# A fused attention backward on one core: normalised o kept in the rows of do, wide projections and transposes, a later dv

## The chip, the core and the metric

The kernel runs on one core of a Trainium2 chip. Five engines work side by side, each through its own queue in order: PE (TensorE, matmuls; its weight loads are listed as PEld), DVE (VectorE), ACT (ScalarE), POOL (GpSimd) and SP (SyncE, which here only issues DMAs). The metric is device time of one execution in microseconds, lower is better.

## The reference

Two attention blocks run on separate inputs, their outputs are laid side by side, and the kernel returns that output and the gradients of all inputs for a given `grad_out`. S = 2048 tokens, D = 448, H = 16 heads of 28 columns, bf16.

```python
# block A: linear attention
qkv = (x @ wqkv) -> q, k, v          # per head
pq, pk = phi(q), phi(k)              # phi(t) = where(t > 0, t + 1, exp(t)) + 1e-6
kv = einsum("bhsd,bhse->bhde", pk, v); z = sum of pk over the tokens
a = (pq @ kv) / (pq . z + 1e-6) @ wo

# block B: multi-query attention, one k and one v for all heads
q = x @ wq; k = x @ wk; v = x @ wv
p = softmax(q k^T * Dh**-0.5)
b = (p v) @ wo

out, vjp = jax.vjp(concat(a, b)); return out, vjp(grad_out)
```

What the change touches is block B. With o = p v (per head, normalised), do = (gradient of b) wo^T and D = rowsum(do * o), its backward needs dv = p^T do, ds = p * (do v^T - D), dq = ds k, dk = ds^T q, the gradient of wo, which is o^T (gradient of b), and the projections of dq, dk, dv.

## The kernel before

Phase A (to about 200 us) computes all of block A. A preparation of block B (`phase_B_pre`) makes q, k and v; q in rows of tokens (`qn`, in the memory of the tile that the trace calls gaT) is stored to DRAM as `qn_d`. Then comes the main loop.

**Main loop.** It works on 64 blocks b; a block is 256 tokens of q (`qc = b // 8`) and two heads (`pair = b % 8`). Each block passes over all 2048 keys in 8 steps of 256 keys, so there are NU = 512 steps u. The program is written out by hand (`tc.manual_schedule`): one pass of `for u in range(NU + 28)` issues work of several ages.

- Scores of step u (`rows_SD`, PE) go to two of three PSUM banks SB; ACT turns them into e with two exps (L888, L932). e (`eT`) is not normalised.
- For w = u - 16, PE makes do v^T into the banks DB. DVE multiplies one head with e (L893); ACT copies the other (L895) and POOL multiplies it (L896). This is ds. DVE transposes it two steps later (L964).
- In odd u PE adds to dk (`dk_m`); in even u it adds to o and dq (`o_dq`) and to dv (`dv_mm`).
- dv needs e with keys and queries exchanged. SP does this by DMA, one `dma_start_transpose` of two steps at a time (L935), into one of 11 buffers `eN`. The four products of block b are issued in the even steps with u mod 8 of 2, 4, 4 and 6, the first one at u = 8b + 18.

Every matmul helper `mmt` places a product on a part of the array (`tile_position`); `mm` uses all of it. All of them appear in the profile as L627 (mmt) or L81 (mm).

**Once per block.** At u = 8b + 9 DVE copies o out of PSUM into `oTs` (L913). At u = 8b + 10 PE transposes it in eight narrow products per block (`onat_T`) into the `spare` bank of SB, which is the first bank that the scores of u + 1 need. `o_norm` then lets DVE copy it into SBUF (L769) and take the reciprocal of the row sums (L770). POOL multiplies them into the normalised `onat` (L774), scales do by the same factor into `don` (L778), and multiplies do with o (L783), which DVE sums to D two steps later. At u = 8b + 14 `don` is transposed for the next ds.

The identity of `onat_T` takes all 128 rows, so rows 64 to 128 of oTs are set to zero once, by a DVE memset at u = 4 (L906).

**Once per eight blocks.** `onat` (256 tokens, all heads) goes two ways: transposed by SP into `oTq` (L924) for the output projection (`out_proj`, in the steps with u mod 64 of 24, 32, 40, 48), and stored by POOL to a DRAM scratch `on_d` (L908). The q rows for dk are loaded by POOL from `qn_d`, four copies, one each at u mod 64 of 30, 38, 46 and 54 (for the first block at u = 2, 4, 6, 8).

**do.** `do_nat` holds do in rows of tokens. It is produced in slots inside the loop (`do_slots`: `do_proj` on PE, `do_copy` on DVE, L858), 20 of them before u = 27 and 12 up to u = 184, those with u a multiple of 8.

**End of the loop.** From u = 512 no scores are left. `post_load` loads the gradient rows (`gb`, L716), the stored o rows (`on`, L720) and the x rows (L727) through SP, into free eT and eN buffers. `gwo` multiplies o and gradient rows for the gradient of wo, in a count per step that the list `GW` gives, from u = 523. After the loop come the products for the gradients of wk, wv, wq and x.

Of the kernel before, what the change touches and what calls it, by code (L numbers as in the profile page):

```python
# [9 lines left out]
ALU = mybir.AluOpType  # L10
AX = mybir.AxisListType
BF16 = mybir.dt.bfloat16
F32 = mybir.dt.float32
# [11 lines left out]
def kernel(  # L25
# [44 lines left out]
    on_d = dpool.tile([S, 512], BF16, name="on_d")  # L70
# [536 lines left out]
    with ExitStack() as cs_:  # L607
        psA = psc.enter_context(tc.tile_pool(name="psAcc", bufs=1, space=bass.MemoryType.PSUM))
        pe_ = cs_.enter_context(tc.tile_pool(name="ceT", bufs=10, side="right"))
        pn_ = cs_.enter_context(tc.tile_pool(name="ceN", bufs=11, side="right"))  # L610
# [5 lines left out]
        pm_ = cs_.enter_context(tc.tile_pool(name="csm", bufs=2, side="right"))  # L616
# [7 lines left out]
        eT, eN, dsT, dsx, qX, onat, don, doT, rl, prod = ({} for _ in range(10))  # L624
# [37 lines left out]
        oTs = pm_.tile([P, 256], F32, name="oTs", bufs=1)  # L662
# [13 lines left out]
        def out_proj(i, c0, c1, ps):  # L676
            for c in range(4):
                for j in range(4):
                    js = slice(32 * j, 32 * j + 32)
                    mmt(ps[js, 0:c1 - c0], oTq[i // 2][:, 4 * (i % 2) + c, js], wo[:, c, c0:c1], (0, 32 * j), c == 0,  # L680
                        c == 3)
# [11 lines left out]
        post = {"gb": [], "on": [], "xb": []}  # L693
# [6 lines left out]
        def post_load(k):  # L700
            if k in (2, 4, 6, 8):
                zero(post["dkvT"][64:128, 256 * k - 512:256 * k])
            if k == 0:
                mix = pq_.tile([P, 4, 2, 512], BF16, name="qX").rearrange("p a b c -> p (a b c)")
                post["dkvT"], post["dkvn"], post["wkvT"] = mix[:, 0:2048], mix[:, 2048:3072], mix[:, 3072:3072 + D]
                zero(post["wkvT"][64:128, :])
                nc.sync.dma_start(post["wkvT"][0:64, :], wkvT_d[:, :])
            i = k % 4
# [5 lines left out]
            elif k < 4:  # L714
# [3 lines left out]
                n = 4 if i < 3 else 2  # L718
                t = by_tokens(pn_.tile([P, 16, P], BF16, name="eN").rearrange("p a b -> p (a b)"))
                nc.sync.dma_start(t[:, 0:n, :], on_d[i * 512:i * 512 + n * P, :].rearrange("(t p) d -> p t d", p=P))  # L720
                post["on"] += [t[:, j, :] for j in range(n)]
                if i == 3:
                    post["on"] += [onat[7][:, j, :] for j in range(2)]
# [6 lines left out]
        def gwo(n0, n1):  # L730
            for n in range(n0, n1):
# [4 lines left out]
                mm(al[:, 0:D], post["on"][st][:, g_ * P:(g_ + 1) * P], post["gb"][st][:, 0:D], start=(st == 0),  # L736
# [8 lines left out]
        GW = [0, 0, 0, 0, 4, 8, 12, 16, 19, 22, 26, 29, 32, 36, 40, 44, 48, 52, 56, 60, 64, 64]  # L745
# [6 lines left out]
        def onat_T(b, bank):  # L752
            onp = bank[:, 0:P].rearrange("p (q h c) -> p q h c", q=2, h=2)
            for qb in range(2):
                for j in range(4):
                    mmt(bank[32 * j:32 * j + 32, qb * 64:qb * 64 + 64], oTs[:, qb * P + 32 * j:qb * P + 32 * j + 32],
                        identF[:, 0:64], (0, 32 * j), True, True)
            onps[b] = onp

        def o_norm(b):  # L760
            onp = onps.pop(b)
            qc, pair, g, hp = blk(b)
            if pair == 0:
                onat[qc] = pm_.tile([P, 2, 512], BF16, name="onat")
            ont = onat[qc]
            cs0 = slice(pair * 64, pair * 64 + 64)
            r_ = pw_.tile([P, 2, 2, 1], F32, name="rl")
            os_ = oTs[:, 0:P].rearrange("p (q h c) -> p q h c", q=2, h=2)
            nc.vector.tensor_copy(out=os_, in_=onp[:, :, :, :])  # L769
            nc.vector.reciprocal(out=r_[:], in_=os_[:, :, :, 0:1])  # L770
            rl[b] = r_
            onv = ont[:, :, cs0].rearrange("p q (h c) -> p q h c", c=32)
            dnv = do_nat[:, 2 * qc:2 * qc + 2, cs0].rearrange("p q (h c) -> p q h c", c=32)
            nc.gpsimd.tensor_tensor(out=onv, in0=os_, in1=r_[:].to_broadcast([P, 2, 2, 32]),  # L774
                                    op=ALU.mult)
# [3 lines left out]

        def do_o(b):  # L780
            qc, pair, g, hp = blk(b)
            prod[b] = pw_.tile([P, 2, 2, 32], F32, name="prod", bufs=1)
            nc.gpsimd.tensor_tensor(  # L783
                out=prod[b][:],
                in0=do_nat[:, 2 * qc:2 * qc + 2, pair * 64:pair * 64 + 64].rearrange("p q (h c) -> p q h c", c=32),
                in1=onat[qc][:, :, pair * 64:pair * 64 + 64].rearrange("p q (h c) -> p q h c", c=32),
                op=ALU.mult)
# [63 lines left out]
        def do_proj(i, h, ps):  # L851
            for c in range(4):
                for j in range(4):
                    js = slice(32 * j, 32 * j + 32)
                    mmt(ps[js, 0:256], gbT[:, i, c, js], woTp[:, c, h * 256:(h + 1) * 256], (0, 32 * j), c == 0, c == 3)
# [7 lines left out]
        with tc.manual_schedule():  # L863
            tc.keep_in_program_order(nc.scalar.activation(out=ex[:], in_=ex[:], func=ACT.Exp))
            for u in range(NU + 28):
# [31 lines left out]
                if u in (2, 4, 6, 8) or u % 64 in (30, 38, 46, 54) and u < 448:  # L897
                    qc, a = (u // 64 + 1, (u % 64 - 30) // 8) if u > 20 else (0, (u - 2) // 2)
# [6 lines left out]
                if u == 4:  # L905
                    nc.vector.memset(oTs[64:128, :], 0.0)  # L906
                if (b := due(u, 14)) is not None and b % 8 == 7 and b < NB - 1:
# [35 lines left out]
                else:  # L943
                    o_dq((u - 2, u - 1), (u - 20, u - 19))
                    for n in {2: (0,), 4: (1, 2), 6: (3,)}.get(u % 8, ()):
                        if 0 <= (b := u // 8 - 2) < NB:
                            dv_mm(b, n // 2, n % 2)
# [120 lines left out]
```

## Time and profile before

| what | us |
|---|---|
| median of 4 runs | 1113.7 |
| lowest and highest of them | 1111.68 and 1118.39 |
| the profiled execution, its time | 1109.44 |
| its span in the profile | 1107.7 |
| main loop, u = 16 to 512 | 262 to 1027 |
| end of the loop, u = 512 to 540 | 1027 to 1071 |
| after the loop | 1071 to 1107.7 |

In the timelines shown below a row has the start in us from the span's beginning, the duration in us, the engine, the line of the kernel, the operation, what is written and read by the program's names, the shape, and how often the row stands for a run of the same kind. In brackets stand the idle time of the engine before it and what ended that time. In the view of one tile a row has minimum, median and maximum duration in ns, and first and last start in us.

### The profile page before, as it was taken

What the parts mean: (1) busy time and instruction counts of PE and PEld (TensorE: products, weight loads), DVE (VectorE), ACT (ScalarE), POOL (GpSimd) and SP (SyncE); (2) the same over time, 40 slices, a digit from 0 to 9 for tenths busy, and PEclk for the clock granted to TensorE, in tenths of its full rate; (3) what the DMA queues carried; (4) which work ended last, traced back from release to release, by engine and by line L of the source; (5) the groups of instructions that cost most, each with busy time, mean ns of one, the idle gap of its engine ahead of it and who ended that gap; (6) DMA issues with size and microseconds to landing.
All of it is one profiled execution on the core that took longest, in us unless ns stands there. A gap on an engine that the chain in (4) does not pass through costs nothing.

```text
span 1107.7 us, 42448 instructions
## 1 busy us (share of the span) xinstructions
PE 1046.6 (94%) x17285; PEld 502.6 (45%) x17285; DVE 892.9 (81%) x1773; ACT 876.6 (79%) x1744; POOL 768.1 (69%) x993
## 2 busy tenths in 40 slices
PE   9999999969999999999999999999899999999898
PEld 5545555435444444444444444444444444444344
DVE  7887400426999999999999999999999999899842
ACT  6453122448999999999999999999999999999521
POOL 6001242225898898889889898888898898888740
PEclk9999999979999999999999999999999999999999
DMA  9869899199999999999999999999999999999992
GB/s 268 147 121 171 171 186 222 34 204 196 182 197 183 187 193 187 187 192 188 190 179 203 193 186 188 191 190 174 194 197 193 197 186 194 178 184 175 248 210 63
DMA packets 674963, 202.89 MB, mean 183 GB/s; under 512 B 649760, under 2 KB 670288, under 8 KB 674768
## 3 DMA queue, kind: packets, MB, share of 16 engines
q1 hardware_dynamic: 662368, 177.03, 99.6%
q0 software_dynamic: 7440, 19.20, 6.7%
q10 hardware_dynamic: 4960, 3.96, 1.2%
q8 instruction: 135, 2.21, 0.8%
q14 instruction: 60, 0.49, 0.2%
HBM read 22.83 MB, written 14.77 MB: 34 GB/s over the span
## 4 chain that ended last, share of the span: by engine, by line
PE 69%; DVE 11%; ACT 10%; DMA 7%; issue 2%; POOL 0%; SPq 0%; DVEq 0%; ACTq 0%
PE dk_acc L627 19%; PE agen L81 13%; PE sps L627 12%; ACT eT L932 8%; PE oq L627 6%; PE dps L627 5%; DMA eN<-eT 5%; PE aacc L81 4%; PE dv_acc L627 4%; DVE dsT L893 3%; PE sps L81 3%; DVE dsx L964 3%; PE sps L800 1%; ACT cp L895 1%; DVE R L916 1%
## 5 line engine op out<-in xcount | busy, mean ns | idle before, releaser
L896 POOL TENSOR_TENSOR dsT<-cp,eT 128x512 bf16<-128x512 bf16 x512 | 589.6, 1157 | 105.0 <-ACT cp L895 93.4
L627 PEld LDWEIGHTS <-R 32*128 32x128 bf16 (+1 forms) x8704 | 227.5, 94 | 293.0 <-issue 259.3
L893 DVE TENSOR_TENSOR dsT<-dps,eT 128x512 bf16<-128x512 f32 x512 | 340.9, 666 | 24.2 <-PE dps L627 18.5
L964 DVE STREAM_TRANSPOSE dsx<-dsT 128x512 f32<-128x512 f32 x512 | 355.6, 695 | 2.1
L888 ACT ACTIVATE eT<-sps 128x512 bf16<-128x512 f32 x512 | 312.0, 609 | 38.0 <-PE sps L627 17.2
L895 ACT ACTIVATE cp<-dps 128x512 bf16<-128x512 f32 x512 | 312.7, 611 | 13.0 <-PE dps L627 11.9
L932 ACT ACTIVATE eT<-sps 128x512 bf16<-128x512 f32 x512 | 318.8, 623 | 0.0
L627 PE MATMUL dk_acc<-dsx,qX 32*32 32x512 bf16 x4096 | 267.6, 375 | 0.0
L627 PE MATMUL dps<-doT,R 32*128 32x256 bf16 x2048 | 247.8, 269 | 5.8 <-ACT cp L895 2.0
L627 PE MATMUL sps<-R,R 32*128 32x256 bf16 (+1 forms) x2240 | 226.3, 274 | 8.7 <-DVE R L858 1.9
L627 PE MATMUL oq<-eT,R 128*32 128x256 bf16 x2048 | 157.8, 275 | 0.0
L627 PE MATMUL oq<-dsT,R 128*32 128x256 bf16 x2048 | 156.3, 274 | 0.1
L627 PEld LDWEIGHTS <-qX 32*32 32x32 bf16 x4096 | 79.6, 89 | 114.5 <-issue 53.8
L627 PE MATMUL dv_acc<-eN,don 128*32 128x512 bf16 x1024 | 101.9, 379 | 7.2 <-DMA eN<-eT 7.0
L397 POOL MEMSET ga<- 64x448 bf16 x2 | 0.9, 470 | 95.7 <-DVE pr L348 82.5
L547 DVE TENSOR_TENSOR osb<-R 32x512 bf16<-32x512 bf16 x4 | 1.7, 413 | 62.1 <-ACT R L544 62.1
L81 PEld LDWEIGHTS <-R 128*128 128x128 bf16 (+1 forms) x361 | 29.5, 99 | 27.7 <-issue 5.6
L627 PE MATMUL sps<-identF,oTs 128*32 128x64 f32 x1024 | 27.6, 225 | 7.5 <-ACT eT L932 0.2
L627 PEld LDWEIGHTS <-don 128*32 128x32 bf16 x1024 | 34.3, 97 | 0.3
L901 POOL DMA_DIRECT2D qX<-qn_d x32 | 18.6, 581 | 16.8 <-DMA qn_d<-gaT 16.8
L774 POOL TENSOR_TENSOR onat<-oTs,rl 128x128 bf16<-128x128 f32 x64 | 25.7, 401 | 6.1 <-DVE rl L770 6.1
L81 PE MATMUL agen<-R,R 128*128 128x448 bf16 x128 | 28.6, 352 | 0.9 <-ACT R L220 0.6
(225 smaller groups left out, 1029.4 us busy)
## 6 DMA issues: line engine op xcount, KB each, us to landing
qX<-qn_d POOLq DMA_DIRECT2D x32, 256.0 KB, 5.1
eN<-eT SPq DMA_TRANSPOSE x256
out_dram<-osb ACTq DMA_DIRECT2D x22, 112.0 KB
qn_d<-gaT SPq DMA_DIRECT2D x2, 1024.0 KB
xa<-in_A_x_dram SPq DMA_DIRECT2D x8, 224.0 KB
ga<-in_grad_out_dram SPq DMA_DIRECT2D x4, 448.0 KB
xa<-in_grad_out_dram POOLq DMA_DIRECT2D x4, 448.0 KB, 6.6
out_dram<-wdq POOLq DMA_DIRECT2D x8, 224.0 KB, 3.6
```

Of the source, the lines that this page charges most:

```text
L81: nc.tensor.matmul(out_ap, lhsT=lhsT, rhs=rhs, start=start, stop=stop, tile_position=(0, 0))
L627: nc.tensor.matmul(out, lhsT=lhsT, rhs=rhs, start=start, stop=stop, tile_position=pos, skip_group_check=True)
L774: nc.gpsimd.tensor_tensor(out=onv, in0=os_, in1=r_[:].to_broadcast([P, 2, 2, 32]), op=ALU.mult)
L800: nc.tensor.transpose(tp2[q:q + 32, qb * P:(qb + 1) * P], don[b][:, qb, h, :], identB[:, :], tile_position=(0, q))
L888: nc.scalar.activation(out=et[:, u % 2, 0, :], in_=sp[0][:, :], func=ACT.Exp, scale=scale)
L893: nc.vector.tensor_tensor(out=dst[:, 0, :], in0=dp[0][:, :], in1=ew[:, w % 2, 0, :], op=ALU.mult)
L895: nc.scalar.activation(out=cp[:, :], in_=dp[1][:, :], func=ACT.Copy)
L896: nc.gpsimd.tensor_tensor(out=dst[:, 1, :], in0=cp[:, :], in1=ew[:, w % 2, 1, :], op=ALU.mult)
L901: nc.gpsimd.dma_start(qX[qc][32 * a:32 * a + 32, :, :, :].rearrange("j b s c -> j b (s c)"), qn_d[qc * 256:(qc + 1) * 256, :].rearrange("( ...
L916: nc.vector.tensor_scalar(out=qT_B[g][64 * hp:64 * hp + 64, qc * 256:(qc + 1) * 256], in0=oq[64:128, 0:256], scalar1=scale, scalar2=None, ...
L932: nc.scalar.activation(out=et[:, u % 2, 1, :], in_=sp[1][:, :], func=ACT.Exp, scale=scale)
L964: nc.vector.transpose(out=dsx[b][:, tp, :, :, :].rearrange("p h t c -> p (h t c)").bitcast(F32), in_=dsT[y][:, :, :].rearrange("p h c -> p ...
```

## The change

It is one edit of the main loop in six parts.

1. The normalised o isn't kept in `onat` any more. DVE takes the reciprocal and the product straight out of PSUM, into oTs (float32). POOL multiplies do with o, makes `don`, and then copies o (as bf16) over the do values that it has just used. The gradient of wo and the transposes for the output projection read o there. The store to `on_d` and its reload are gone, and so is their pool; oTs now lies in the pool of the outputs (`pp_`).
2. The o transpose is two real transposes of 64 rows by 128 columns. The memset of the upper rows of oTs is gone.
3. Output projection and do projection use the whole array, four matmuls of 128 columns of weights instead of sixteen of 32.
4. The q loads are issued two at a time, at u mod 64 of 38 and 54 (at u = 2 and 8 at the start).
5. eN has 12 buffers, and the dv products are issued two steps later, in the even steps with u mod 8 of 4, 6, 6 and 0.
6. The products for the gradient of wo begin at u = 519, and some of the tiles used after the loop come out of eN buffers instead of a q buffer.

```diff
-    on_d = dpool.tile([S, 512], BF16, name="on_d")
...
-        pn_ = cs_.enter_context(tc.tile_pool(name="ceN", bufs=11, side="right"))
+        pn_ = cs_.enter_context(tc.tile_pool(name="ceN", bufs=12, side="right"))
...
-        pm_ = cs_.enter_context(tc.tile_pool(name="csm", bufs=2, side="right"))
...
-        oTs = pm_.tile([P, 256], F32, name="oTs", bufs=1)
+        oTs = pp_.tile([P, 256], F32, name="oTs", bufs=1)
...
         def out_proj(i, c0, c1, ps):
             for c in range(4):
-                for j in range(4):
-                    js = slice(32 * j, 32 * j + 32)
-                    mmt(ps[js, 0:c1 - c0], oTq[i // 2][:, 4 * (i % 2) + c, js], wo[:, c, c0:c1], (0, 32 * j), c == 0,
-                        c == 3)
+                mm(ps[:, 0:c1 - c0], oTq[i // 2][:, 4 * (i % 2) + c, :], wo[:, c, c0:c1], start=(c == 0), stop=(c == 3))
...
         def post_load(k):
-            if k in (2, 4, 6, 8):
-                zero(post["dkvT"][64:128, 256 * k - 512:256 * k])
-            if k == 0:
-                mix = pq_.tile([P, 4, 2, 512], BF16, name="qX").rearrange("p a b c -> p (a b c)")
...
+            if k == 4:
+                post["dkvT"], mix = (pn_.tile([P, 16, P], BF16, name="eN").rearrange("p a b -> p (a b)") for _ in range(2))
...
+            if 5 <= k < 9:
+                zero(post["dkvT"][64:128, 512 * k - 2560:512 * k - 2048])
...
-                n = 4 if i < 3 else 2
-                t = by_tokens(pn_.tile([P, 16, P], BF16, name="eN").rearrange("p a b -> p (a b)"))
-                nc.sync.dma_start(t[:, 0:n, :], on_d[i * 512:i * 512 + n * P, :].rearrange("(t p) d -> p t d", p=P))
-                post["on"] += [t[:, j, :] for j in range(n)]
-                if i == 3:
-                    post["on"] += [onat[7][:, j, :] for j in range(2)]
...
-                mm(al[:, 0:D], post["on"][st][:, g_ * P:(g_ + 1) * P], post["gb"][st][:, 0:D], start=(st == 0),
+                mm(al[:, 0:D], do_nat[:, st, g_ * P:(g_ + 1) * P], post["gb"][st][:, 0:D], start=(st == 0),
...
-        GW = [0, 0, 0, 0, 4, 8, 12, 16, 19, 22, 26, 29, 32, 36, 40, 44, 48, 52, 56, 60, 64, 64]
+        GW = [0, 2, 4, 7, 10, 13, 16, 19, 22, 25, 28, 31, 34, 37, 40, 44, 48, 52, 56, 60, 64, 64]
...
             for qb in range(2):
-                for j in range(4):
-                    mmt(bank[32 * j:32 * j + 32, qb * 64:qb * 64 + 64], oTs[:, qb * P + 32 * j:qb * P + 32 * j + 32],
-                        identF[:, 0:64], (0, 32 * j), True, True)
+                nc.tensor.transpose(onp[:, qb, :, :].rearrange("p h c -> p (h c)"), oTs[0:64, qb * P:(qb + 1) * P],
+                                    identF[0:64, 0:64], tile_position=(0, 0))
...
         def o_norm(b):
...
-            nc.vector.tensor_copy(out=os_, in_=onp[:, :, :, :])
-            nc.vector.reciprocal(out=r_[:], in_=os_[:, :, :, 0:1])
+            nc.vector.reciprocal(out=r_[:], in_=onp[:, :, :, 0:1])
+            nc.vector.tensor_tensor(out=os_, in0=onp[:, :, :, :], in1=r_[:].to_broadcast([P, 2, 2, 32]), op=ALU.mult)
             rl[b] = r_
...
-            nc.gpsimd.tensor_tensor(out=onv, in0=os_, in1=r_[:].to_broadcast([P, 2, 2, 32]),
-                                    op=ALU.mult)
+            nc.gpsimd.tensor_tensor(out=prod[b][:], in0=dnv, in1=os_, op=ALU.mult)
             dn = pw_.tile([P, 2, 2, 32], BF16, name="don", bufs=3)
             don[b] = dn
             nc.gpsimd.tensor_tensor(out=dn[:], in0=dnv, in1=r_[:].to_broadcast([P, 2, 2, 32]), op=ALU.mult)
+            nc.gpsimd.tensor_copy(out=dnv, in_=os_)
...
         def do_proj(i, h, ps):
             for c in range(4):
-                for j in range(4):
-                    js = slice(32 * j, 32 * j + 32)
-                    mmt(ps[js, 0:256], gbT[:, i, c, js], woTp[:, c, h * 256:(h + 1) * 256], (0, 32 * j), c == 0, c == 3)
+                mm(ps[:, 0:256], gbT[:, i, c, :], woTp[:, c, h * 256:(h + 1) * 256], start=(c == 0), stop=(c == 3))
...
-                if u in (2, 4, 6, 8) or u % 64 in (30, 38, 46, 54) and u < 448:
-                    qc, a = (u // 64 + 1, (u % 64 - 30) // 8) if u > 20 else (0, (u - 2) // 2)
+                for a in {2: (0, 2), 8: (1, 3)}.get(u, ()) or {38: (0, 2), 54: (1, 3)}.get(u % 64, ()) * (u < 448):
+                    qc = u // 64 + (u > 20)
...
-                if u == 4:
-                    nc.vector.memset(oTs[64:128, :], 0.0)
-                if (b := due(u, 14)) is not None and b % 8 == 7 and b < NB - 1:
-                    nc.gpsimd.dma_start(on_d[b // 8 * 256:(b // 8 + 1) * 256, :].rearrange("(q p) c -> p q c", p=P),
-                                        onat[b // 8][:, :, :])
...
-                        nc.sync.dma_start_transpose(oTq[q_][:, :, :], onat[q_][:, :, :].rearrange("p q c -> p (q c)"))
+                        nc.sync.dma_start_transpose(oTq[q_][:, :, :], do_nat[:, 2 * q_:2 * q_ + 2, :].rearrange("p q c -> p (q c)"))
...
-                    for n in {2: (0,), 4: (1, 2), 6: (3,)}.get(u % 8, ()):
-                        if 0 <= (b := u // 8 - 2) < NB:
+                    for n in {4: (0,), 6: (1, 2), 0: (3,)}.get(u % 8, ()):
+                        if 0 <= (b := (u - 20) // 8) < NB:
                             dv_mm(b, n // 2, n % 2)
```

## Prediction

> **What bounds the kernel now.** I read the page first, then the timeline of one block of the main loop engine by engine, then SP's own timeline, and last the two ends of the loop. The page names no single bound:
>
> ```profile
> PE 1046.6 (94%) x17285; PEld 502.6 (45%) x17285; DVE 892.9 (81%) x1773; ACT 876.6 (79%) x1744; POOL 768.1 (69%) x993
> ```
>
> The main loop (u from 16 to 512, 262 to 1027 us) is 69% of the span. Its beat is read from the starts of ACT's first exp (L888), one per u; here u is 230 to 237, so u mod 8 is 6, 7, 0, 1, 2, 3, 4, 5:
>
> ```profile
> 590.03 0.62 ACT L888 ACTIVATE eT<-sps 128x512 bf16<-128x512 f32 x1
> ...
> 591.50 0.61 ACT L888 ACTIVATE eT<-sps 128x512 bf16<-128x512 f32 x1
> ...
> 592.95 0.63 ACT L888 ACTIVATE eT<-sps 128x512 bf16<-128x512 f32 x1
> ...
> 594.67 0.60 ACT L888 ACTIVATE eT<-sps 128x512 bf16<-128x512 f32 x1
> ...
> 596.12 0.62 ACT L888 ACTIVATE eT<-sps 128x512 bf16<-128x512 f32 x1
> ...
> 597.74 0.60 ACT L888 ACTIVATE eT<-sps 128x512 bf16<-128x512 f32 x1
> ...
> 599.18 0.62 ACT L888 ACTIVATE eT<-sps 128x512 bf16<-128x512 f32 x1
> ...
> 600.71 0.60 ACT L888 ACTIVATE eT<-sps 128x512 bf16<-128x512 f32 x1
> ```
>
> Odd slots take 1.45 us: three ACT passes start 0.48 apart, so ACT is the floor. The even slots take 1.47 (slot 6), 1.72 (0, with an output projection), 1.62 (2, with the o transpose) and 1.53 (4). There PE, or the PSUM bank that DVE must empty, keeps ACT waiting. A block is thus 12.1 us, but 765 us for 62 blocks is 12.34. The rest is in a queue:
>
> ```profile
> L935 SPq DMA_TRANSPOSE eN<-eT x256: 1334/3005/5892, 236.6 to 1034.7; - x128
> ...
> 551.84 32.12 SPq L935 DMA_TRANSPOSE eN<-eT  x11
> ...
> 580.97 31.07 SPq L935 DMA_TRANSPOSE eN<-eT  x10
> ...
> 1027.43 0.60 ACT L932 ACTIVATE eT<-sps 128x512 bf16<-128x512 f32 x1
> ```
>
> SP issues the transposes of e back to back: eleven in 32.12 us (2.92 each) while no copy is about, ten in 31.07 (3.11) beside two q loads and a store. The loop asks for one per two u, 3.08 us. Counted off against L932, a transpose starts some 4 us after its tile is ready at u = 20, some 10 us after it from u = 180 on, and the last still 6.7 us after. Since it lands 5 us later and dv needs it 10 to 11 u (16 us) after the tile was ready, dv then waits. Slot 2, where dv reads first, has a median of 1.63 us but a mean of 1.9 from u = 192: about 0.3 x 40 blocks, 12 to 14 us with the rest. So ACT with PE's stretched slots, and the DMA stream, are two bounds nearly level.
>
> **Start and end of the loop.**
>
> ```profile
> 245.78 0.27 DVE L906 MEMSET oTs<- 64x256 f32 x1 [10.18 <-DMA qn_d<-gaT]
> ...
> 246.56 1.05 PE L627 MATMUL dps<-R,R 128*32 128x256 bf16 x16 [8.58 <-DVE R L858]
> ...
> 1038.80 0.46 SPq L720 DMA_DIRECT2D eN<-on_d  x1
> ...
> 1044.29 0.93 PE L81 MATMUL sps<-eT,eN 128*128 128x448 bf16 x4 [1.56 <-DMA eN<-on_d]
> ```
>
> A memset at u = 4 holds DVE 10 us until a DMA has read the tile that lay there before, and PE and ACT stand behind it. At the end the first product with reloaded o rows waits 1.56 us.
>
> **The change, part by part** (the sum is against this execution: span 1107.7, time 1109.4; the median of the runs shown, 1113.7, is 4.3 above it, and I carry differences over).
>
> Start: the memset goes, and oTs moves to another pool. By the tiles' sizes its new place is past the old one of gaT; the small tiles (rl, don) still lie there, and u = 10, reached at about 243 us, would wait until 245.8. So of 10 us I count 7 (bounds 0 and 10). **-7.**
>
> DMA: seven stores of on_d (256 KB) leave POOL's queue and four reloads leave SP's. A store is not seen alone; the nearest row is the q load of the same size: (3.11 - 2.92) x 10 = 1.9 us for two loads and a store half as large, some 0.8 each. Around the store at 543.03, with the oTq transpose beside it, five transposes take 2 us more than that transpose explains. I take 1.0, bounds 0 and 2. The Trainium skill ("DMA: Bandwidth & Descriptors", Anatomy of one DMA) prices what is moved at bytes / 436 GB/s, 0.6 us here: 4 us of stream by the rule, 7 by the row; I keep the row. POOL also loses seven issues of 0.75 us, which it had time for (105 us idle in L896).
>
> dv later by two u, with the twelfth buffer: the stream may be 3 us later before dv waits. With the 7 us this should take nearly all of the waits: **-13**, if the loop does not itself become slower.
>
> What dv does in its new slots is the price. Four matmuls of 512 columns are 0.215 us of PE. Slot 6 now has two: there PE sets the next scores (dv from 590.67, scores 591.08, exp 591.50), so +0.21. Slot 4 loses one, but there the exp waits for a DVE pass that is late (L893 at 599.63): 0. In slot 2 dv goes, but
>
> ```profile
> 593.14 0.57 PE L627 MATMUL sps<-wo,oTq 128*32 128x224 bf16 x16
> ...
> 593.81 0.39 DVE L686 CAST ot<-sps 128x224 bf16<-128x224 f32 x1 [0.19 <-PE sps L627]
> ...
> 596.85 0.29 DVE L769 COPY oTs<-sps 128x128 f32<-128x128 f32 x1
> 597.18 0.18 DVE L770 RECIPROCAL rl<-oTs 128x4 f32<-128x4 f32 x1
> ```
>
> the bank that the next scores need was free after the copy at 597.14; now a reciprocal (0.18) and a multiply that waits for it (0.3, from the 128x140 multiply out of PSUM at 296 ns) both read it, until about 597.37. Scores started at 597.31, so between -0.1 (PE alone) and +0.12 (bank): I take +0.06. The two wide transposes for 16 narrow matmuls have no row; anything up to 0.3 us hides behind that bank. Slot 0 gets a dv and the wide projection. The width: 16 matmuls in four column groups take 0.38 us, four wide ones of 224 columns the same 4 x 0.096. The Trainium skill ("TensorE: Matmul & The Clock Gate", The mechanism) lets a weight load overlap running matmuls only in other row groups. Then every wide load (98 ns) would stand in the open, 0.39 us in each of 40 projections of the loop, 16 us in all. This trace's wide products (four of 448 columns in 0.93 us, starts 0.19 apart, which is the streaming alone) show them hidden, so I count 0. But the array drains at each change of tile shape: PEld idles 0.1 us past the streaming, and the narrow projection shared the shape of o and dq behind it. PE was ready at 594.08 while the bank came free at 594.20; +0.215 + 0.11 makes 594.41, so +0.15 in 40 blocks, none in the 22 without a projection: +0.09 on average. Sum 0.21 + 0.06 + 0.09 = 0.36, x 62 = **+22** (bounds +5 and +30).
>
> At nothing: POOL's multiply, don and the new copy (some 0.3 us between its 84- and 448-element copies) are 0.1 us less than before per block, and POOL waits for ACT. oTq now waits for POOL's third operation instead of its first, 0.8 us later on SP's queue with the transposes behind it, hidden while SP is 4 us or more behind; up to 6 us in all if not. Two q loads at once hold POOL 1.16 us, which L964 two u later covers, and push the stream by 2 us at a time, inside the 3 us gained; they are first read 37 u later.
>
> End: the stall of 1.6 us goes, and the products start four u earlier, in slots paced by DVE. They still need gradient rows that SP issues only behind its last transpose. **-2** (bounds -4 and +2).
>
> Sum: -7 - 13 + 22 - 2 = 0; the start and the waits are surer than the slots, so I round to -2: 1111.7.
>
> **Rivals.** (1) *The DMA stream alone decides.* If the slots cost a third of what I count, ACT runs ahead until dv waits again, and the end is tied to the stream: last transpose 7 us earlier, rows for the products at about 1035 instead of 1044, but four more u (5.4 us) behind them: -4 to -10, 1104 to 1110, most at 1106. For it: SP is never idle from 250 us on. Against: PE starts every even slot late already. (2) *Slower: the two dv in slot 6.* If don_T, o, dq and eight dv matmuls do push every block by 0.21 and the bank in slot 2 by 0.12 or more, the block is 0.45 longer, +28 against -7 - 13 + 2: +10, 1124. It decides where the loop's own pace passes 3.1 us per transpose, for then nothing of the freed DMA time comes back. For it: slot 6's exp follows PE's scores with no slack. Against: odd slots have 0.1 us of PE slack. (3) *The change doesn't act:* in-place writes into the do rows might make the copies of do (L858) or the oTq transposes wait; they touch other rows, so I give it little, inside (2).
>
> **Numbers.** A difference of 0.5% (5.6 us) is about what these runs can tell. No net change 0.37 (around 1111.7, own range 1106 to 1118), the stream 0.35, slower 0.28. The first gives 0.05 of its chance to each side, the stream 0.08 of its to no change: faster 0.32, same 0.35, slower 0.33. Range 1099 to 1126.
>
> **What would show it.** Right: no DVE wait near 245 us, u = 16 some 7 us earlier; no wait of dv on eN; slot 6 near 1.7, slot 4 unchanged, slot 2 at 1.65 to 1.75, slot 0 1.85 with a projection; SP's last transpose about 1028 to 1032. Wrong: slots 6 and 0 unchanged (then the stream decides), wide weight loads in the open, or a new wait at u = 10 as long as the old one.

## The result and the profile after

The kernel after takes 1108.95 us (median of 44 runs, 1103.1 to 1120.6) against 1113.94 us of the kernel before. The ratio is 0.9982, 95% interval 0.9965 to 0.9999: 2 us or 0.2%, inside the 0.5% called "the same" in the prediction (forecast: 1111.7 us, range 1099 to 1126). The ratio compares only the executions within 1.5% of the fastest of their kernel, which is why it lies nearer to 1 than the quotient of the two medians (0.9955). The profiled execution took 1108.93 us, its span is 1107.2 us (before 1107.7). Busy times have hardly moved, and what is looked for lies between the rows:

```profile
PE 1048.3 (95%) x15645; PEld 485.6 (44%) x15645; DVE 898.0 (81%) x1772; ACT 881.4 (80%) x1744; POOL 757.1 (68%) x986
```

The beat is read as before, from the starts of ACT's first exp (now L861). Here u is 228 to 235, so u mod 8 is 4, 5, 6, 7, 0, 1, 2 and 3:

```profile
590.11 0.62 ACT L861 ACTIVATE eT<-sps 128x512 bf16<-128x512 f32 x1
591.70 0.60 ACT L861 ACTIVATE eT<-sps 128x512 bf16<-128x512 f32 x1
593.15 0.62 ACT L861 ACTIVATE eT<-sps 128x512 bf16<-128x512 f32 x1
594.84 0.60 ACT L861 ACTIVATE eT<-sps 128x512 bf16<-128x512 f32 x1
596.29 0.62 ACT L861 ACTIVATE eT<-sps 128x512 bf16<-128x512 f32 x1
598.13 0.60 ACT L861 ACTIVATE eT<-sps 128x512 bf16<-128x512 f32 x1 [0.25 <-PE dps L625]
599.59 0.62 ACT L861 ACTIVATE eT<-sps 128x512 bf16<-128x512 f32 x1
601.26 0.60 ACT L861 ACTIVATE eT<-sps 128x512 bf16<-128x512 f32 x1
```

Slot 6 (593.15 to 594.84) takes 1.69 us, slot 0 with an output projection 1.84, slot 2 1.67. The medians from u = 32 to the end of the loop, from the same rows (slot 4 goes to and fro between about 1.5 and 1.6 us, so its mean is given):

| slot (u mod 8) | before | after |
|---|---|---|
| 0 with an output projection | 1.71 | 1.84 |
| 0 without a projection | 1.48 | 1.48 |
| 2 | 1.62 | 1.68 |
| 4 | 1.58 | 1.53 |
| 6 | 1.51 | 1.70 |
| odd | 1.45 | 1.45 |

PE's timeline shows where slots 6, 0 and 2 get their length. A row is again start, duration, engine, line, operation, tiles and shape:

```profile
593.80 0.69 PE L625 MATMUL dv_acc<-eN,don 128*32 128x512 bf16 x8
...
594.42 0.28 PE L625 MATMUL sps<-R,R 32*128 32x256 bf16 x2
...
596.47 0.54 PE L80 MATMUL sps<-wo,oTq 128*128 128x224 bf16 x4
...
597.39 0.39 PE L625 MATMUL dv_acc<-eN,don 128*32 128x512 bf16 x4
...
597.71 0.28 PE L625 MATMUL sps<-R,R 32*128 32x256 bf16 x2
...
600.85 0.28 PE L625 MATMUL sps<-R,R 32*128 32x256 bf16 x2 [0.21 <-DVE oTs L754]
```

In slot 6 eight matmuls of dv stand straight in front of the scores that the next exp needs; in slot 0 a wide projection and four of dv. In slot 2 the scores wait for DVE's multiply. The waits view gives that wait 62 times, once a block (us in all, times, longest), and the wait of dv on the transposed e, which stood there with 7.0 us before, is gone from it:

```profile
PE sps L625 <- DVE oTs L754: 14.5, 62, 1.4
...
DVE rl L753 <- DMA qn_d<-gaT: 2.4, 1, 2.4
```

The second line is what is left of the 10.2 us of the old memset: the first `rl` waits at u = 10, as the prediction had it, until 246.17 us.

```profile
246.17 0.18 DVE L753 RECIPROCAL rl<-sps 128x4 f32<-128x4 f32 x1 [2.41 <-DMA qn_d<-gaT]
```

SP's timeline at the end of the loop: the last transpose of e starts at 1029.78 instead of 1034.7 us, and the gradient rows follow at once.

```profile
1029.78 1.72 SPq L902 DMA_TRANSPOSE eN<-eT  x1
1031.60 1.12 SPq L711 DMA_DIRECT2D eT<-in_grad_out_dram  x1
```

Against L899 a transpose now starts 7 to 12 us after its tile is ready at u = 8 to 20, but only some 1 us after it from u = 128 on (median; 9.4 us before). So the stream of transposes does not set the pace of this kernel any more; PE's slots do.

By stages of the two traces: the time to u = 0 is 0.8 us longer, u = 0 to 16 is 5.5 shorter, the loop from u = 16 to 511 takes 771.2 instead of 764.8 (6.4 longer), the rest 79.0 instead of 81.2. Sum: -0.5 us, the difference of the spans.

### The profile page after: what moved, and what is told of

Read it like the earlier page. It is cut to its first block, busy times and chain, and to the rows that moved or that the text cites. A ratio compares the mean times of both kernels' runs of the same rounds, so it can differ in the third digit from the quotient of the medians.

```text
span 1107.2 us, 39147 instructions
## 1 busy us (share of the span) xinstructions
PE 1048.3 (95%) x15645; PEld 485.6 (44%) x15645; DVE 898.0 (81%) x1772; ACT 881.4 (80%) x1744; POOL 757.1 (68%) x986
## 4 chain that ended last, share of the span: by engine, by line
PE 55%; DVE 28%; ACT 8%; issue 6%; DMA 2%; SPq 0%; POOL 0%; DVEq 0%; ACTq 0%; POOLq 0%
PE agen L80 13%; PE dk_acc L625 12%; DVE dsx L931 11%; DVE dsT L866 9%; PE sps L80 6%; ACT eT L899 5%; PE oq L625 5%; PE sps L625 5%; PE aacc L80 4%; PE dps L625 4%; PE dv_acc L625 3%; DVE R L884 2%; DVE oTs L881 2%; DVE oTs L754 2%; PE sps L775 1%
## 5 line engine op out<-in xcount | busy, mean ns | idle before, releaser
L861 ACT ACTIVATE eT<-sps 128x512 bf16<-128x512 f32 x512 | 311.8, 609 | 34.2 <-PE dps L625 11.4
L625 PEld LDWEIGHTS <-R 32*128 32x128 bf16 (+1 forms) x8192 | 197.8, 94 | 300.3 <-issue 268.7
L899 ACT ACTIVATE eT<-sps 128x512 bf16<-128x512 f32 x512 | 319.0, 623 | 0.0
L625 PE MATMUL dps<-doT,R 32*128 32x256 bf16 x2048 | 253.1, 270 | 13.0 <-DVE dsT L866 7.7
L625 PE MATMUL sps<-R,R 32*128 32x256 bf16 x2048 | 217.9, 275 | 16.1 <-DVE oTs L754 14.5
L625 PE MATMUL dv_acc<-eN,don 128*32 128x512 bf16 x1024 | 96.3, 379 | 0.0
L80 PEld LDWEIGHTS <-R 128*128 128x128 bf16 (+1 forms) x553 | 46.1, 100 | 46.2 <-issue 18.6
L884 DVE TENSOR_SCALAR R<-oq 64x256 bf16<-64x256 f32 x64 | 27.3, 426 | 2.0
L744 PE MATMUL sps<-identF,oTs 64*128 64x64 f32 x128 | 21.3, 247 | 7.5
```

Source lines behind the costliest of these rows:

```text
L80: nc.tensor.matmul(out_ap, lhsT=lhsT, rhs=rhs, start=start, stop=stop, tile_position=(0, 0))
L625: nc.tensor.matmul(out, lhsT=lhsT, rhs=rhs, start=start, stop=stop, tile_position=pos, skip_group_check=True)
L744: nc.tensor.transpose(onp[:, qb, :, :].rearrange("p h c -> p (h c)"), oTs[0:64, qb * P:(qb + 1) * P], identF[0:64, 0:64], tile_position=(0 ...
L861: nc.scalar.activation(out=et[:, u % 2, 0, :], in_=sp[0][:, :], func=ACT.Exp, scale=scale)
L884: nc.vector.tensor_scalar(out=qT_B[g][64 * hp:64 * hp + 64, qc * 256:(qc + 1) * 256], in0=oq[64:128, 0:256], scalar1=scale, scalar2=None, ...
L899: nc.scalar.activation(out=et[:, u % 2, 1, :], in_=sp[1][:, :], func=ACT.Exp, scale=scale)
```

## The experiments

Each was timed beside the kernel before, and ratios are against it. "Lag" is the time from the end of the second exp of a tile to the start of its transpose; with a lag of several us SP issues back to back.

### Undoing single parts

**dv where it was before**, in the kernel after:

```diff
-                    for n in {4: (0,), 6: (1, 2), 0: (3,)}.get(u % 8, ()):
-                        if 0 <= (b := (u - 20) // 8) < NB:
+                    for n in {2: (0,), 4: (1, 2), 6: (3,)}.get(u % 8, ()):
+                        if 0 <= (b := u // 8 - 2) < NB:
```

> The changed kernel with its dv products issued in the old slots again (u mod 8 of 2, 4, 4, 6, from u = 8b + 18), everything else kept. Theory (two bounds nearly level: ACT's beat stretched by what PE does in the even slots, and the stream of e transposes): slot 6 falls from 1.70 to 1.50 us and slot 0 with a projection from 1.84 to about 1.73; slot 2 stays at 1.68 to 1.75, because its dv runs while PE waits for the bank anyway; slot 4 rises from 1.53 to 1.57. A block is 12.1 to 12.2 us by the slots, but the stream allows about 12.25, so some wait of dv on eN returns. Loop 7 to 12 us shorter than in the changed kernel; about 1101, ratio to the kernel before 0.988 to 0.992. Rival A (the place of dv costs nothing, PE has slack there): as the changed kernel, 0.998. Rival B (the early place was why dv waited, so all waits of the kernel before return): slot 2 mean above 1.85, 0.996 or more.

Measured: 1108.77 us, ratio 0.9943 (0.9912 to 0.9973), short of the 0.988 to 0.992 that was expected. The direction is right: slot 6 is back at 1.50 and slot 0 with a projection at 1.68. But slots that are some 0.28 us a block shorter would be worth 17 us, 1.5%, and the time is only 0.4% below that of the kernel after, with intervals that overlap. In the trace (of an execution of 1117.2 us) slot 2 has a mean of 1.9 beside its median of 1.68, which was rival B's sign, and dv waits for the transposed e again:

```profile
PE dv_acc L625 <- DMA eN<-eT: 17.1, 6, 6.7
```

Of these 4.7 us fall at u = 18. So the stream sets the pace once the slots do not, although the stores are gone.

**The narrow projections**, in the kernel after (the same for `do_proj`):

```diff
-                mm(ps[:, 0:c1 - c0], oTq[i // 2][:, 4 * (i % 2) + c, :], wo[:, c, c0:c1], start=(c == 0), stop=(c == 3))
+                for j in range(4):
+                    js = slice(32 * j, 32 * j + 32)
+                    mmt(ps[js, 0:c1 - c0], oTq[i // 2][:, 4 * (i % 2) + c, js], wo[:, c, c0:c1], (0, 32 * j), c == 0,
+                        c == 3)
```

> The changed kernel with output and do projections in sixteen narrow matmuls again, everything else kept. Theory (a drain of 0.11 us at the extra change of tile shape, the streaming equal): slot 0 with a projection falls from 1.84 to about 1.73, 40 blocks, so 4.4 us less in the loop and about 1 us less in the 20 do projections before it; about 1104, ratio 0.993 to 0.995. Rival A (wide and narrow cost the same, slot 0 is set by the dv that came): 0.998. Rival B (wide is quicker, since it has a quarter of the loads and matmuls): slower than the changed kernel, 1.000 or more.

Measured: 1111.46 us, 0.9987 (0.9958 to 1.0016), a miss. Slot 0 with a projection falls to 1.76 us as expected, but the lag stays at some 10 us (median from u = 128 on) and the waits come back, the longest of them in steps with u mod 64 of 60, behind the second pair of q loads:

```profile
PE dv_acc L625 <- DMA eN<-eT: 9.7, 5, 5.2
```

With no store of o left in it, this kernel's stream is as slow as before's: 782 us from the fifth transpose to the last, before 779.

**No store of o**, in the kernel before (the reload at the end reads `qn_d` instead, so the gradient of wo is of other data):

```diff
-                if (b := due(u, 14)) is not None and b % 8 == 7 and b < NB - 1:
-                    nc.gpsimd.dma_start(on_d[b // 8 * 256:(b // 8 + 1) * 256, :].rearrange("(q p) c -> p q c", p=P),
-                                        onat[b // 8][:, :, :])
```

> The kernel before without the seven stores of o to on_d; the four reloads stay but read qn_d instead, so the gradient of wo is made from other rows. Theory (each store takes about 1 us of the stream of e transposes, and the stream is one of the bounds): the waits of dv on eN shrink, slot 2's mean from u = 192 on falls from 1.9 to about 1.75; the loop is 5 to 7 us shorter; about 1108, ratio 0.994 to 0.996. Rival (the store runs beside the transposes at no cost, and the waits come from the q loads and the pace of the transposes alone): 1.000.

Measured: 1099.93 us, 0.988 (0.9832 to 0.9927): 13.4 us for seven stores, 1.9 us each (1.2 to 2.7 by the interval), twice what was expected. dv's waits fall from 7.0 to 2.6 us. This is the largest single gain in the change, and the kernel after does not show it.

**Only oTs moved**, in the kernel before:

```diff
-        oTs = pm_.tile([P, 256], F32, name="oTs", bufs=1)
+        oTs = pp_.tile([P, 256], F32, name="oTs", bufs=1)
```

> The kernel before with one word changed: the tile oTs comes from the pool of the outputs, past the memory that the store of q reads. Theory: the 10 us stand of DVE at u = 4 goes, u = 16 comes 7 to 9 us earlier, but the stream of e transposes starts no earlier and is then behind from the beginning, so that dv waits for eN from the first blocks on and most of the gain is lost in the loop: 1 to 4 us gained in all, ratio 0.996 to 0.999. Rival (parts add up, the loop runs at its own pace): 8 us gained, 0.993.

Measured: 1114.51 us, 1.0023 (0.9999 to 1.0047): no gain, not even the 1 to 4 us expected. Counted from u = 0, u = 16 does come 6.0 us earlier in the trace, but u = 32 comes 0.9 later. SP's timeline of the kernel before, and after it that of this run, tell why:

```profile
240.58 60.32 SPq L935 DMA_TRANSPOSE eN<-eT  x17
```

```profile
238.83 62.64 SPq L935 DMA_TRANSPOSE eN<-eT  x17
```

The same seventeen transposes are over at 300.9 and at 301.5 us. The first of them are what u = 18 waits for (PE's timeline of this run):

```profile
262.28 0.58 PE L627 MATMUL dv_acc<-eN,don 128*32 128x512 bf16 x1 [3.57 <-DMA eN<-eT]
```

Steps that start earlier only wait for the same stream two blocks on.

### The q loads by twos

The remaining suspect was a part that the prediction had put at nothing. Fifteen transposes from u mod 64 = 29 on, in which the four q loads of a block fall, take 47.1 and 47.4 us (means over six q blocks) in the kernel before and in the one without the store, but 48.5 in the kernel after and 49.9 in the one with narrow projections, both with pairs. Four kernels test it. First the kernel before without the store, and with pairs:

```diff
-                if u in (2, 4, 6, 8) or u % 64 in (30, 38, 46, 54) and u < 448:
-                    qc, a = (u // 64 + 1, (u % 64 - 30) // 8) if u > 20 else (0, (u - 2) // 2)
+                for a in {2: (0, 2), 8: (1, 3)}.get(u, ()) or {38: (0, 2), 54: (1, 3)}.get(u % 64, ()) * (u < 448):
+                    qc = u // 64 + (u > 20)
```

> The kernel before without the stores of o (as in the run without them, which came out at 0.988: the reload at the end reads q rows instead of o rows, so the gradient of wo is of other data), and now with the q loads issued two at a time, as the kernel after has them. Theory A: pairs of q loads hold up the stream of transposes more than single ones do. Summed over the transposes from u mod 64 = 29 to 57, fifteen intervals take 47.1 and 47.4 us in two kernels with single loads, and 49.9 and 51.7 us in two kernels with pairs, so 2.5 us or more for each of the seven q blocks, some 17 us in all. The time should rise from 0.988 to 1.000 to 1.005 of the kernel before, and the fifteen intervals to about 50 us. Theory B (the prediction's: pairs cost the stream nothing, the difference came from the other changes): it stays at 0.988, within 0.003.

Measured: 1115.61 us, 1.0024 (0.9999 to 1.0049), as theory A has it. The whole gain of the removed stores is gone again: 1.0024 - 0.988 is 1.4%, or 16 us. The fifteen transposes of one q block on SP, without pairs and with them:

```profile
680.81 47.05 SPq L931 DMA_TRANSPOSE eN<-eT  x15
```

```profile
689.49 51.51 SPq L931 DMA_TRANSPOSE eN<-eT  x15
```

Means over six q blocks are 47.4 and 50.7 us. POOL's row at the first pair of that block, and the transpose on SP behind it, 6.2 us long where 2.9 is usual:

```profile
695.66 1.13 POOL L900 DMA_DIRECT2D qX<-qn_d  x2
```

```profile
698.90 6.22 SPq L931 DMA_TRANSPOSE eN<-eT  x1
```

The waits of dv, first without pairs and then with them:

```profile
PE dv_acc L626 <- DMA eN<-eT: 2.6, 5, 0.8
```

```profile
PE dv_acc L626 <- DMA eN<-eT: 9.4, 12, 3.3
```

The other three put single loads (the reverse of that diff) into the kernel after, alone and beside the parts tried above. **Single loads alone:**

> The kernel after with the q loads issued one at a time, as before. Theory A (pairs hold up the stream, but in the kernel after the steps of PE and ACT are longer still, 12.4 to 12.6 us a block against some 12.3 of the stream, so the stream is hidden): only the first 32 steps, where dv waited, gain: 0.995 to 0.998 of before, that is 0 to 4 us below the kernel after, and the slots from u = 64 on as in after (slot 6 1.70, slot 0 1.84 with a projection, slot 2 1.68). Theory C (the stream still sets the pace of the kernel after somewhere): 0.988 or less. Theory B (pairs cost nothing): 0.998, as the kernel after.

Measured: 1106.04 us, 0.9956 (0.9937 to 0.9975), 3 us below the kernel after; slots unchanged, lag 0 to 3 us from u = 128 on. In the kernel after itself the pairs are nearly hidden, as the prediction said, because its slots are longer than the stream.

**Single loads and narrow projections:**

> The kernel after with narrow projections (16 matmuls of 32 columns of weights, as before) and with single q loads. With the narrow projections alone the waits of dv on the transposed e had come back (9.7 us) and the time was 0.9987. Theory A (these waits come from the stream that the pairs hold up): they go, the slots alone decide, with slot 0 at 1.76 instead of 1.84 with a projection, 40 times: 3 to 4 us below the kernel after with single q loads, 0.991 to 0.994 of before. Theory B (pairs cost nothing): 0.9985.

Measured: 1105.74 us, 0.9947 (0.9924 to 0.9971). The waits of dv shrink from 9.7 to 1.3 us, but against single loads alone the narrow projections bring nothing that these intervals can tell, though slot 0 with a projection is 1.76 instead of 1.84. The lag is 3 to 10 us from u = 128 on in this trace, so the stream is near there too. (The fifteen transposes take 49.0 us here and 49.9 with pairs; what the single loads change is the waits.)

**Single loads and dv early:**

> The kernel after with dv issued where it was before (u mod 8 of 2, 4, 4, 6) and with single q loads. With dv early alone the time was 0.9943 and dv waited on the stream. Its slots sum to 12.29 us where nothing waits. Theory A (pairs hold up the stream by some 17 us in all): the waits shrink to a few us, 0.984 to 0.988 of before (1096 to 1101 us), and the transposes take 3.07 us on average from the 4th to the last. Theory B (pairs cost nothing): 0.994, as with dv early alone, 3.09 us or more.

Measured: 1097.0 us, 0.9852 (0.9801 to 0.9902), as theory A has it. It is the fastest kernel of the study, 1.3% below the kernel after. Against dv early with pairs it is 0.9% faster (there the first four loads are in pairs too); against single loads with dv late 1.0%, some 12 us. In the profiled execution (1090.49 us) its engines do the work of the kernel after in a span of 1088.8 us, 18 us less (the page's row), and one wait of dv is left (the waits):

```profile
PE 1049.7 (96%) x15645; PEld 496.7 (46%) x15645; DVE 892.1 (82%) x1772; ACT 875.7 (80%) x1744; POOL 758.3 (70%) x986
```

```profile
PE dv_acc L625 <- DMA eN<-eT: 2.7, 1, 2.7
```

### What in the pairs costs the time

Two variants of that fastest kernel, with the first four loads single. Two and two, but 3 us apart:

```diff
+                if u in (2, 4, 6, 8) or u % 64 in (38, 40, 54, 56) and u < 448:
+                    qc, a = (u // 64 + 1, {38: 0, 40: 2, 54: 1, 56: 3}[u % 64]) if u > 20 else (0, (u - 2) // 2)
```

> The kernel of 0.985 (after, dv early, single q loads) with the four q loads of a block at u mod 64 of 38, 40, 54 and 56 instead of 30, 38, 46 and 54: two and two as in after, but 3 us apart instead of in one step. The first four loads stay at u = 2, 4, 6, 8. Theory A1 (two copies in flight at the same moment are what holds up the stream): 0.983 to 0.988, as with single loads. Theory A2 (two copies within some transposes are too many, whether or not they overlap): 0.992 or more, half or more of the way to the 0.9943 of the pairs. A copy takes 5 to 7 us to land, so under A1 a part of the loss, up to a half, may remain.

And all four in one step:

```diff
+                for a in {2: (0,), 4: (1,), 6: (2,), 8: (3,)}.get(u, ()) or {38: (0, 1, 2, 3)}.get(u % 64, ()) * (u < 448):
+                    qc = u // 64 + (u > 20)
```

> The same kernel (0.985) with all four q loads of a block at once, at u mod 64 of 38; the first four stay at u = 2, 4, 6, 8. The bytes are the same. If what is paid grows with the number of copies in flight together (A1), four at once cost more than two pairs: the time passes the 0.9943 of the pairs, 0.995 to 1.005. If only the count of stretches with a copy mattered (B1), there is one stretch a block instead of four, and the time is 0.985 or below.

Measured: spaced 1099.85 us, 0.9869 (0.9829 to 0.9908); four at once 1114.62 us, 0.9999 (0.9968 to 1.003). With single loads (0.9852) and pairs (0.9943) this makes a series that rises with the number of copies started together: the same bytes cost 1.5% more all at once than one at a time. Slot 2, where dv reads first, has a median of 1.68 us in all four traces, but means (from u = 32 on) of 1.69 with single loads, 1.79 spaced, 1.93 with pairs and 1.91 with four: dv waits. The intervals of the spaced and the single loads overlap, so of A1 and A2 it is A1 that holds for most of the loss; a small loss from the nearness of two copies is not excluded. (A q load has a median of 5 to 7 us from issue to landing, so two that start 3 us apart still overlap in part.) POOL's row for four loads in one step, and the transpose behind it on SP:

```profile
697.75 2.23 POOL L874 DMA_DIRECT2D qX<-qn_d  x4
```

```profile
699.41 7.38 SPq L902 DMA_TRANSPOSE eN<-eT  x1
```

In each of the seven q blocks the slowest transpose beside the four loads takes at least 7.1 us until the next one starts, up to 16.9.

The pages show where that time lies. Their row for POOL's DMA queue gives packets, MB, and the time that the packets took as a share of the span of all 16 DMA engines; here for single loads, spaced, pairs (dv early) and four at once:

```profile
q0 software_dynamic: 6880, 17.37, 6.2%
...
q0 software_dynamic: 6880, 17.37, 6.6%
...
q0 software_dynamic: 6880, 17.37, 7.0%
...
q0 software_dynamic: 6880, 17.37, 7.4%
```

The same packets and bytes take 68, 72, 78 and 83 us (share times span), so one packet takes longer the more loads start together: those of 4 KB in the loop have means of 274, 294, 349 and 385 ns. The 15 us between the first and the last are close to the 16 us by which the times differ. The kernel before without the store shows the same: 5.9% with single loads, 6.8% with pairs. In the kernel after, where SP does not issue back to back, pairs give 6.1% and single loads 5.9%. Why a packet takes longer, and how much of its time it only waits beside the transposes' packets, was not shown.

### The two remaining prices of the slots

**One dv product moved from slot 6 to slot 4**, with single loads and narrow projections:

```diff
-                    for n in {4: (0,), 6: (1, 2), 0: (3,)}.get(u % 8, ()):
+                    for n in {4: (0, 1), 6: (2,), 0: (3,)}.get(u % 8, ()):
```

> The kernel after with single q loads, narrow projections, and dv at u mod 8 of 4, 4, 6 and 0: the two dv products in one step lie in slot 4, where the exp waits for DVE, instead of slot 6, where it waits for PE. If slot 6 of the kernel after was long because of its second dv, and slot 4 has the room: slot 6 back from 1.70 to 1.50, slot 4 from 1.53 to at most 1.58, slot 0 1.76 with a projection and 1.48 without, slot 2 1.68; 0.15 us a block less than the run with single loads and narrow projections (0.9947), 62 times, so 0.985 to 0.988 of before. The rival: slot 4 takes over what slot 6 loses (1.70), and it stays at 0.994.

Measured: the slots are as expected (6: 1.48, 4: 1.55 on average, 2: 1.68, 0 with a projection 1.77), so the second dv product made slot 6 long and slot 4 has room. The time is not: 1112.13 us over all its 22 runs, and 0.9955 (0.9928 to 0.9983) in the comparison. The profiled execution was its fastest, 1099.35 us, with a lag of 6 to 13 us from u = 128 on; what holds up the others was not seen. The lag says that the stream is near again, but waits of dv are only 2.3 us in this trace, so why the shorter slots are not paid out stays open.

**DVE copies o out of PSUM first**, in the fastest kernel:

```diff
-            nc.vector.reciprocal(out=r_[:], in_=onp[:, :, :, 0:1])
-            nc.vector.tensor_tensor(out=os_, in0=onp[:, :, :, :], in1=r_[:].to_broadcast([P, 2, 2, 32]), op=ALU.mult)
+            nc.vector.tensor_copy(out=os_, in_=onp[:, :, :, :])
+            nc.vector.reciprocal(out=r_[:], in_=os_[:, :, :, 0:1])
+            nc.vector.tensor_tensor(out=os_, in0=os_, in1=r_[:].to_broadcast([P, 2, 2, 32]), op=ALU.mult)
```

> The kernel of 0.985 with DVE copying o out of PSUM first, then the reciprocal and the product in SBUF, as before: one DVE operation more a block (some 0.3 us), but the bank that the next scores need is free after the first of them. If slot 2 of the kernel after is held by that bank: slot 2 from 1.68 to 1.62, and no more wait of PE on oTs; slot 4 may grow by up to 0.05 as DVE is late there. In time 0.982 to 0.985, less than the 3.7 us of the slots, since the stream of transposes is nearly as slow. If the bank is not what holds slot 2, it stays at 1.68 and the time at 0.985 or 0.986.

Measured: the question has its answer, slot 2 falls from 1.68 to 1.64 us, so that bank held it. (PE has no wait on oTs left, but there were only three, 0.8 us in all, in the fastest kernel, where dv fills that time.) But the time is 1149.56 us, 1.0315 (1.0274 to 1.0356). Slot 3 has grown from 1.45 us to a mean of 2.2, slot 4 from 1.54 to 1.82. Most of it is the new multiply. In the groups of the fastest kernel the multiply out of PSUM, and in this one the multiply in SBUF (busy us, mean ns):

```profile
L754 DVE TENSOR_TENSOR oTs<-sps,rl 128x128 f32<-128x128 f32 x64 | 18.7, 292 | 2.2
```

```profile
L755 DVE TENSOR_TENSOR oTs<-oTs,rl 128x128 f32<-128x128 f32 x64 | 61.5, 961 | 2.2
```

The mean hides two kinds: 18 of the 64 take 0.29 us, 45 take 0.8 us or more. From the fourth block on slot 3 follows them: 2.46 or 2.47 us where the multiply is long, 1.45 to 1.52 where it is short. Per block the multiply is 0.67 us longer in the mean and the added copy takes 0.27, together nearly the 1.0 us a block by which the loop is longer than in the fastest kernel's trace. The timelines of DVE and then POOL around one of the long ones:

```profile
621.24 1.24 DVE L755 TENSOR_TENSOR oTs<-oTs,rl 128x128 f32<-128x128 f32 x1
```

```profile
621.18 1.16 POOL L870 TENSOR_TENSOR dsT<-cp,eT 128x512 bf16<-128x512 bf16 x1 [0.32 <-ACT cp L869]
```

It began 0.06 us after POOL's multiply and ended 0.14 us after POOL's end (622.34). The 29 long ones among the first forty all end 0.14 to 0.15 us after POOL's pass. Where DVE comes first, POOL's pass is the longer one:

```profile
608.70 0.29 DVE L755 TENSOR_TENSOR oTs<-oTs,rl 128x128 f32<-128x128 f32 x1
```

```profile
608.70 1.30 POOL L870 TENSOR_TENSOR dsT<-cp,eT 128x512 bf16<-128x512 bf16 x1 [0.31 <-ACT cp L869]
```

This is what the Trainium skill ("SBUF — State Buffer", SBUF: two separate sides) states: a DVE operation with two SBUF inputs and a GpSimd operation that reads SBUF exclude each other for a whole instruction. The multiply of the kernel after reads one input from PSUM and is free of it: 47 of its 64 rows run beside a multiply of POOL, and all 64 take 0.29 us.

## Why the prediction was right, and where it was not

The forecast number and range held, and so did the picture of longer slots against fewer waits of dv. Part of the agreement is luck: of the stream the prediction counted 7 us for the stores and nothing for the pairs, where the runs show 13 and 16. The two errors nearly cancel, and the longer slots of the kernel after hide what is left.

**Start, -7.** The trace has -5.5 us from u = 0 to 16, and the new wait stood where it was put. Yet the move alone gained nothing in time (1.0023): what it wins before u = 16 is lost to the stream at u = 18 to 32, since the transposes of the first tiles end no earlier. So the step is wrong that counts this gain for the whole kernel by itself. In the kernel after, where dv comes later, 4 of the 5.5 us are still there at u = 32.

**DMA, 1.0 us a store (0 to 2).** Measured 1.9 us each, at the upper bound. Both hints that the prediction had were too low, the estimate from the bytes (0.6) by a factor of three.

**Two q loads at once, at nothing.** This is the term that was mis-sized as a price of the stream: 16 us in all in a kernel that the stream binds, about 1 us for each of 16 pairs (14 in the loop, two at its start). The cover that the prediction named, the 3 us of a later dv, is real: in the kernel after, only 3 us remain to be gained from single loads. So the sum came out, but most of the later dv is used up to hide the pairs.

**Waits of dv, -13.** They are gone from the list of waits. The slots of the table make 0.28 us a block (0.13 x 40 / 62 + 0.06 - 0.05 + 0.19), 18 us in 62 blocks, and the loop is 6.4 us longer, so some 12 us of waits went: right. Slot 2 agrees: before, its mean lay 0.20 us above its median, 12 us in 62 blocks; now the two are equal.

**Slots, +22 (5 to 30).** Measured +18, as worked out above. Slot 6 was put at +0.21 and is +0.19, and the run with one dv there shows 1.48. Slot 4 was put at 0 and is -0.05. Slot 2 was put at +0.06 and is +0.06, and the copy out of PSUM first shows that the bank is the cause. Slot 0 with a projection was put at +0.15 and is +0.13. The runs split this last one: wide without dv 1.68, narrow with dv 1.76, narrow without dv 1.71, both 1.84. So the wide form alone costs nothing (-0.03) and dv alone 0.04, but both together 0.13. That fits the prediction's picture of PE being ready a little ahead of the bank: either alone is covered or nearly so, the two are not. The single terms were not measured apart from each other inside the slot.

**Wide weight loads, hidden.** Right: with them in the open a slot with a projection would be 0.39 us longer, and the wide one without dv is no longer than the narrow one. The measurement decides: the rule that a weight load overlaps running matmuls only in other row groups (the Trainium skill, "TensorE: Matmul & The Clock Gate", The mechanism; the same section also lets a load go ahead that targets the background weight buffer) puts no such time into this loop.

**POOL and oTq, at nothing.** No wait on oTq stands in the list of the kernel after. Weight loads wait for POOL's `don` as before (9.4 us in 44 waits, before 7.5 in 34, none over 0.6), and behind POOL's new copy stands one wait of 1.0 us. **End, -2.** Measured -2.2; the products begin three steps earlier (before at u = 522), not four.

**The rivals.** The stream alone (1) does not decide in the kernel after, whose lag falls to some 1 us; it does where dv is early and the loads come in pairs (17.1 us of waits). The slower case (2) had its mechanism, slot 6, but the block grew by 0.3 and not 0.45 us. (3) did not show but for that one wait.

Where the gain went, then: the removed stores are worth 13 us. The pairs cost 16 us where the stream sets the pace; the later dv hides most of that and costs 0.3 us a block in slots 6 and 0 (0.19, and 1.84 - 1.68 in 40 of 62 blocks). With single loads and dv where it was, the other parts of the change are worth 1.5%. The stores alone gave 1.2%, and these intervals can't tell the rest from nothing.

## What to carry to other kernels

Where a DMA stream runs back to back, price every copy beside it by how many start together, not by its bytes alone; spread loads over the steps, and look at the stream's intervals around each and at the time that the page gives for their packets. Before work is moved later to give a stream slack, look which slots have room: here a dv product before a step's critical matmuls cost nearly its full length (0.19 us in slot 6), and one in a step that waits for another engine anyway cost next to nothing (0.01 in slot 4). A gain at the start of a pipeline counts only if its slowest queue starts earlier too.

## What was not expected of the hardware

- Four copies of 256 KB (q loads) beside the transposes cost 1.5% more of the time when started in one step than when started in four: 0.9999 against 0.9852. One transpose in each q block took 7.1 us or more there, 2.9 is usual, and the loads' 4 KB packets took 385 ns instead of 274.
- A DVE multiply of 128x128 in float32 takes 0.29 us from PSUM and from SBUF alike, but up to 1.25 us from SBUF while POOL's 1.16 us multiply runs. It was 0.67 us longer a block in the mean, and the kernel, which also has a copy of 0.27 us a block more, 4.7% longer (1.0315 against 0.9852).
